# Retention and an exact-GELU MLP on one core: ten warm-up products instead of seven, whole products in the opening's gaps, first loads in another order

## The chip, the core and the metric

The kernel runs on one core of a Trainium2 chip. A core has a matrix engine (TensorE, PE in the profile; its weight loads are listed as PEld), a vector engine (VectorE, DVE), a scalar engine (ScalarE, ACT), a general engine that here mostly issues loads (GpSimd, POOL), and a queue engine for stores (SyncE, SP). They run side by side and wait for each other by semaphores. Sixteen DMA engines move data between the main memory and the core's own memory. The metric is the device time of one execution in microseconds (us), the median of several runs.

## The reference

For 8 batches and 8 heads, 576 positions of 64 numbers, the reference takes retention scores with a decay for each head, multiplies them with the values, lays the heads beside each other, and puts the 4608 rows of 512 through an MLP with an inner width of 2048 and the exact GELU:

```
scores = (1 / sqrt(64)) * q @ k.T                   # per batch and head
gamma  = 1 - 2 ** (-5 - head)
Dmat   = where(i >= j, gamma ** (i - j), 0)
x      = (scores * Dmat) @ v                        # heads side by side: [4608, 512]
h      = x @ w_in                                   # [4608, 2048]
out    = (0.5 * h * (1 + erf(h / sqrt(2)))) @ w_out # [4608, 512]
```

All inputs and the output are float32 in main memory.

## The kernel before

**Tiles.** Positions are cut into pieces of 128 (the fifth has 64), and a unit is one such piece of one batch with all heads. There are 4608 / 128 = 36 units; four make a block of 512 tokens for the MLP, nine blocks in all. The units of the first block, called tiles 0 to 3 here, are the first pieces of batches 0 to 3. A later piece of the same batch needs a state carried over from the pieces before it; the first pieces need none.

**Steps of a unit.** The queries and keys of one unit are transposed on TensorE (`turn`, line 456 for its products) into PSUM and copied out as `qkT` (line 487 on VectorE, 489 on ScalarE). `scores` multiplies them; `masked` (line 623) multiplies the scores in PSUM with the decay (`near`) into `ret`. `inner` multiplies `ret` with the values; `evacuate` converts its result to `x`. `scaled_v` (line 649) weights the values for the carried state, and `state` multiplies them with the keys. `mlp1` multiplies `x` with `w_in` two blocks of 128 inner columns at a time, ScalarE applies the GELU (line 802) into `g_all`, `mlp2` multiplies with `w_out`. Later blocks use a form of both with fewer products. All products go through `mm` (line 452), transposes through `mm_turn` (line 456).

**Opening.** q and k of tile 0 and its values are loaded as float32 by SyncE and ScalarE (line 149) and converted on VectorE (`early<-q`, `early<-k`, `early<-first_v`). All other loads are issued by POOL in the order of the list `ORDER`: in `q1`, `k2` or `v3` the number is the tile, `wi` and `wo` are eighths of `w_in` and `w_out`, `io` builds constants. They land in the tile `early` (line 368), `w_in` (line 311) and `w_out` (line 326). Eight loads are in flight at most; a further one waits until the load eight places ahead of it has landed. The list, as far as it concerns the opening:

```
"wi0 io q1 k2 k1 wi7 v1 q2 k3 v0 wi1 wi6 q3 wo2 v2 wi5 v3 wi3 wi4 wo1 wi2 ..."
```

(`v0` does nothing here, since it came as float32.)

**Warm-up products.** TensorE begins with `N_WARM` products of 128 x 512 on a tile of zeros whose result nobody reads. `warm(n)` puts n more of them where the plan sees a gap. They do no work that the output needs.

**The plan.** The whole program is written out by one loop in Python before it is launched. It keeps a planned time for each engine (`T["pe"]` and so on), planned landing times (`land`) and planned durations, and at each step picks the next piece of work for TensorE that is ready by these times. Nothing of it runs on the chip: only the order it gives does. Four constants that the change touches: `HOT` is the planned time up to which a product counts twice its duration, `WARM_TO` the time up to which gaps are filled, `RATE` says how far scores may run ahead of the MLP, `JOIN` allows scores a little more lead directly after an `inner`. The fill at the loop's end reads:

```
gap = min(waits) - now
if now < WARM_TO and gap > (0.6 if now < HOT else 0.2 if now < 16 else 0.5):
    warm(int(gap / 0.6) + WPLUS if now < HOT else max(1, round(gap / 0.23)) + WPLUS)
```

Of the kernel before, what the change touches and what calls it, by code (L numbers as in the profile page):

```python
# [17 lines left out]
def kernel(  # L18
# [64 lines left out]
    VH_ACT = [4, 22, 1]  # L83
    N_XB = 4
    AHEAD = 13
    RATE = 4.6
    STORE_AT = 62.0
    CROWD = 66.0
    STATE10 = 32.0
    HOT = 7.5  # L90
    FETCH = 5.0
    ARRIVE = 5.6
    WPLUS = 0
    WARM_TO = 24.0
    JOIN = 0
    JOIN_SB = 0.0
    VISIT = 4
    LEAD = 5.0
# [4 lines left out]
    N_V = 6  # L103
    MASK_ACT = 99.0
    V0_HW = 1
    N_WARM = 7
    MSK_AT = 24.0
    HK = N_DF // 2

# [11 lines left out]
    T = dict.fromkeys(("pe", "act", "dve", "pool", "sp"), 0.0)  # L121
# [115 lines left out]
    land = {}  # L237
# [22 lines left out]
    def ring_free(tag):  # L260
        n = RINGS[tag][1]
        return len(taken[tag]) < n or taken[tag][-n]()

    def all_loaded():
        return not ORDER and next_load[0] >= N_G

# [102 lines left out]
            land[what, i] = sw_dma(0.88, 0.9) if j is not None else sw_dma(0.68, 0.5)  # L369

    tiles_of(0)
    land["q", 0], land["k", 0] = 4.65, 5.2
    if V0_HW:
        land["v", 0] = 7.45
    cast_due = {("q", 0): (loaded[0][0][0], first["q32"]), ("k", 0): (loaded[0][0][1], first["k32"])}
    if V0_HW:
        cast_due["v", 0] = (loaded[0][1], first["first_v"])
    ORDER = ("wi0 io q1 k2 k1 wi7 v1 q2 k3 v0 wi1 wi6 q3 wo2 v2 wi5 v3 wi3 wi4 wo1 wi2 wo3 wo0 wo4 wo5 k4 q4 wo7 "
             "q5 wo6 v4 dq2 k5 q6 k7 k6 q7 q8 q9 n4 v6 k8 k9 v8 q10 k11 n8 n6 k10 dq3 q11 q12 v10 dq0 q13 dq4 k12 "
             "k13 n10 n12 v12").split()  # L380

    def next_order():
        item = ORDER.pop(0)
        what = item.rstrip("0123456789")
        load(what, int(item[len(what):] or 0))
# [5 lines left out]
    def reload():  # L391
        if next_load[0] < N_G:
            g = groups[next_load[0]]
            ORDER.extend([f"{what}{i}" for what in "qk" for i in g] + [f"{what}{g[0]}" for what in ("vn" if len(g) > 1 else "v")])
            next_load[0] += 1
# [18 lines left out]
    def bank(shape, dtype, name):  # L414

        now = T["pe"]
        def rank(x):
            y = banks[banks.index(x) ^ 1]
            return free_at[x] > now, y not in held and free_at[y] <= now, free_at[x]
        b = min((x for x in banks if x not in held), key=rank)  # L420
        held.add(b)
        return b, view(b, shape[1:], dtype)
# [19 lines left out]
    def release(b, when):  # L442
        held.remove(b)
        free_at[b] = when
# [5 lines left out]
    def mm(*a, **k):  # L450
        count[0] += 2.004
        nc.tensor.matmul(*a, **k)  # L452
# [5 lines left out]
    def place(n):  # L458
        return (n - 194.0) // 256, (n - 194.0) % 256

    def fetch_at(n):

        at = place(count[0])[1]
        wait = piece[0] + FETCH - (256 - at) * 0.0075 if at + n >= 256 else 0.0
        return 0.0 if T["pe"] < 20.0 else wait
# [4 lines left out]
    def pe(dur, to="full"):  # L470
        if mode[0] != to:
            T["pe"] += 0.05 if mode[0][:4] == to[:4] == "row4" else 0.11
            mode[0] = to
        dur *= 2.0 if T["pe"] < HOT else 1.0
        new, old = place(count[0])[0], place(count[1])[0]
        if new > old:
            turn_at = T["pe"] + dur * (1 - place(count[0])[1] / max(1.0, count[0] - count[1]))
            wait = max(0.0, piece[0] + FETCH - turn_at) if T["pe"] > 20.0 else 0.0
            piece[0] = turn_at + wait
            T["pe"] += wait  # L480
        count[1] = count[0]
        T["pe"] += dur
        return T["pe"] + DRAIN
# [709 lines left out]
    def fire():  # L1193
        now = T["pe"]
        while ORDER and T["pool"] <= now + 1.5:
            next_order()
# [33 lines left out]
    def warm(n):  # L1230
        b, t = bank([128, 512], FP32, "warm")
        for _ in range(n):
            mm(t, lhsT=zeros[:, :128], rhs=zeros, start=True, stop=True)
        pe((0.32 if T["pe"] < HOT else 0.2158) * n)
        release(b, T["pe"])

    def attend(*ns):
# [17 lines left out]
    def s_ready(early=0):  # L1255
        n = group_of[nA]
        g = groups[n]
        if n < nT and n not in [x[0] for x in apart_due] and g[-1] // 4 <= tM1 + N_XB - 1 and nA + len(g) <= AHEAD + early + RATE * b1:
            return sg[n]["T"]
        return 1e9  # L1260
# [7 lines left out]
    T["pe"] = 1.3  # L1268
    for _ in range(N_WARM):
        b, t = bank([128, 512], FP32, "warm")  # L1270
        mm(t, lhsT=zeros[:, :128], rhs=zeros, start=True, stop=True)
        release(b, 0.0)
    T["pe"] = 1.3 + 0.62 * N_WARM
    while True:
        fire()
        now = T["pe"]
# [16 lines left out]
        if nB < nA:  # L1293

            n = group_of[nB]
# [15 lines left out]
        if nA < N_U:  # L1311
            n = group_of[nA]
            g = groups[n]
            if T["dve"] <= now + (SB + JOIN_SB if after_a else SB) and nA - nB <= 2:
                acts.append((max(s_ready(JOIN if after_a else 0), fetch_at(64 if n >= 4 else 0), free_time(0, len(g))), "S"))
        if nT < 4 + NPE and nT <= group_of[min(nA, N_U - 1)] + 3 and (nT < 4 or not half or ring_free("tk")):
# [13 lines left out]
        if due:  # L1330
# [8 lines left out]
            elif kind == "S":  # L1339
                n = group_of[nA]  # L1340
# [40 lines left out]
        if not waits:  # L1381
            break
        gap = min(waits) - now
        if now < WARM_TO and gap > (0.6 if now < HOT else 0.2 if now < 16 else 0.5):
            warm(int(gap / 0.6) + WPLUS if now < HOT else max(1, round(gap / 0.23)) + WPLUS)
        T["pe"] = max(T["pe"], min(waits))
    while stores:
        put()
# [31 lines left out]
```

## Time and profile before

| What | Value |
|---|---|
| median of three runs | 292.75 us |
| the three runs | 293.8, 292.75, 291.52 us |
| profiled execution, first to last instruction (its span) | 288.7 us |
| TensorE busy in the span | 279.1 us (97%) |
| VectorE, ScalarE, POOL busy | 229.5, 178.8, 136.2 us |
| granted TensorE clock, mean of the span | 1.000 |

The profile is of one execution. Its page gives the span from the first to the last instruction and not the whole time of that execution; the runs lie 2.8 to 5.1 us above the span. The rows of a timeline are merged: neighbours of one engine with the same line and tiles stand in one row with their count. In brackets stands how long the engine was idle before the row's first instruction, and what ended that wait. A product's length reaches to its modelled end, so that the lengths of neighbours overlap; the distance of their starts is what they cost in a stream.

### The profile page before, as it was taken

The numbers are of one execution on the slowest core, as the hardware profiler recorded it, in microseconds if no ns is written. First come the engines' busy times: TensorE is split into PE (matmuls) and PEld (weight loads), VectorE is DVE, ScalarE is ACT, GpSimd is POOL, SyncE is SP. The second block draws the span as 40 slices with busy tenths as digits, with TensorE's granted clock in tenths as the row PEclk, the third lists the DMA queues.
The fourth block names the chain that finished last, engine by engine and source line by source line (L and its number), as shares of the span: only waits on it lengthen the run. The fifth ranks groups of instructions, "written<-read, shape, count | busy, mean of one in ns | idle before, by whom it ended". The sixth has DMA issues, their size and how long they took to land.

```text
span 288.7 us, 9727 instructions
## 1 busy us (share of the span) xinstructions
PE 279.1 (97%) x4138; PEld 212.5 (74%) x4162; DVE 229.5 (80%) x384; ACT 178.8 (62%) x400; POOL 136.2 (47%) x205
## 2 busy tenths in 40 slices
PE   6899999999999999999999999999999999999994
PEld 2478767888667766666766766777888888888883
DVE  5564289897964799968996799897996998899861
ACT  7355537998378767778578866655645455555421
POOL 8956868996899777678688820000000000000000
PEclk9999999999999999999999999999999999999999
DMA  9999999999989999999999960302020202101114
GB/s 155 170 183 202 185 163 203 201 124 150 116 98 135 140 169 116 184 133 190 163 122 185 82 104 3 77 2 75 0 75 0 76 3 73 73 2 73 39 55 128
DMA packets 109131, 31.96 MB, mean 111 GB/s; under 512 B 85792, under 2 KB 104736, under 8 KB 109088
## 3 DMA queue, kind: packets, MB, share of 16 engines
q0 software_dynamic: 100400, 21.12, 83.2%
q1 hardware_dynamic: 7264, 9.51, 9.9%
q10 hardware_dynamic: 1424, 0.72, 0.9%
q8 instruction: 32, 0.52, 0.7%
q14 instruction: 11, 0.09, 0.1%
HBM read 42.99 MB, written 9.44 MB: 182 GB/s over the span
## 4 chain that ended last, share of the span: by engine, by line
PE 95%; DMA 2%; issue 1%; DVE 0%; POOL 0%; ACT 0%; POOLq 0%; DVEq 0%
PE psum L452 93%; DMA early<-in_q_dram 2%; PE psum L456 1%; POOL w_in L311 0%; DVE qkT L487 0%; DVE o_sb L884 0%; ACT t L489 0%; POOL val L188 0%; POOLq L188 0%; DVEq L487 0%; POOLq L1404 0%; POOL pos L190 0%
## 5 line engine op out<-in xcount | busy, mean ns | idle before, releaser
L452 PE MATMUL psum<-x,w_in 128*128 128x256 bf16 (+2 forms) x716 | 116.8, 303 | 1.6 <-issue 0.8
L452 PEld LDWEIGHTS <-w_in 128*128 128x128 bf16 x736 | 68.1, 98 | 26.1 <-issue 0.3
L452 PEld LDWEIGHTS <-g_all 128*128 128x128 bf16 x576 | 55.6, 98 | 15.1 <-issue 0.6
L452 PE MATMUL psum<-w_out,g_all 128*128 128x256 bf16 (+1 forms) x438 | 58.6, 280 | 0.0
L799 ACT ACTIVATE g_all<-psum 128x512 bf16<-128x512 f32 x64 | 37.7, 594 | 22.8 <-PE psum L452 22.5
L452 PEld LDWEIGHTS <-s 128*128 128x128 bf16 x408 | 39.3, 98 | 8.5
L346 POOL DMA_DIRECT2D k_ld<-in_k_dram x64 | 35.1, 566 | 18.1 <-DMA q_ld<-in_q_dram 10.3
L645 ACT ACTIVATE vh<-v_ld,dv 128x128 bf16<-128x128 bf16 (+1 forms) x144 | 42.2, 379 | 0.0
L628 DVE TENSOR_TENSOR ret<-psum,msk 128x1024 bf16<-128x1024 f32 (+1 forms) x32 | 35.6, 1150 | 7.3 <-PE psum L452 7.2
L1013 ACT ACTIVATE g_all<-t 128x512 bf16<-128x512 f32 x36 | 22.6, 630 | 29.0 <-DVE t L1021 28.9
L346 POOL DMA_DIRECT2D q_ld<-in_q_dram x64 | 35.3, 570 | 2.0 <-DMA v_ld<-in_v_dram 0.9
L452 PE MATMUL psum<-wt,s 128*128 128x256 bf16 x272 | 34.3, 273 | 0.0
L489 ACT COPY t<-psum 128x256 f32<-128x256 f32 (+1 forms) x46 | 20.0, 436 | 21.8 <-PE psum L452 21.5
L884 DVE TENSOR_TENSOR o_sb<-psum,t 128x256 f32<-128x256 f32 x51 | 21.4, 420 | 12.0 <-ACT t L489 6.3
L1021 DVE TENSOR_TENSOR t<-psum,t 128x512 f32<-128x512 f32 x36 | 24.7, 689 | 6.1 <-ACT t L489 4.2
L487 DVE COPY t<-psum 128x512 f32<-128x512 f32 (+1 forms) x41 | 22.6, 558 | 2.9 <-PE psum L452 2.9
L802 ACT ACTIVATE g_all<-psum 128x512 bf16<-128x512 f32 (+1 forms) x36 | 19.3, 549 | 8.0 <-PE psum L452 7.7
L771 DVE TENSOR_TENSOR x<-psum,dqT 128x1024 bf16<-128x1024 f32 (+1 forms) x18 | 19.4, 1095 | 1.1 <-PE psum L452 1.1
L452 PE MATMUL psum<-x,ws 128*128 128x256 bf16 x144 | 19.5, 273 | 0.0
L357 POOL DMA_DIRECT2D v_ld<-in_v_dram x14 | 16.3, 1167 | 4.0 <-ACT g_all L799 2.0
L452 PE MATMUL psum<-wt,g_all 128*128 128x256 bf16 x136 | 17.5, 273 | 0.5 <-ACT t L489 0.5
L452 PE MATMUL psum<-w_out,s 128*128 128x256 bf16 x136 | 17.5, 273 | 0.0
(100 smaller groups left out, 325.9 us busy)
## 6 DMA issues: line engine op xcount, KB each, us to landing
out_dram<-o_sb SPq DMA_DIRECT2D x31, 256.0 KB, 2.4
v_ld<-in_v_dram POOLq DMA_DIRECT2D x14, 256.0 KB, 5.5
q_ld<-in_q_dram POOLq DMA_DIRECT2D x48, 64.0 KB, 5.1
k_ld<-in_k_dram POOLq DMA_DIRECT2D x48, 64.0 KB, 4.5
kn_ld<-in_k_dram POOLq DMA_DIRECT2D x12, 256.0 KB, 6.1
w_in<-in_moe_w_in_dram POOLq DMA_DIRECT2D x8, 256.0 KB, 8.1
w_out<-in_moe_w_out_dram POOLq DMA_DIRECT2D x8, 256.0 KB, 9.5
k_ld<-in_k_dram POOLq DMA_DIRECT2D x4, 128.0 KB, 7.8
```

Of the source, the lines that this page charges most:

```text
L346: nc.gpsimd.dma_start(qk["qk".index(what)][p0:p0 + 32, 0:HP * per].rearrange("p (h x) -> p h x", h=HP), {"q": q, "k": k}[what][2 * bp + jj ...
L452: nc.tensor.matmul(*a, **k)
L487: nc.vector.tensor_copy(dst, src)
L489: nc.scalar.copy(dst, src)
L628: nc.vector.tensor_tensor(both.rearrange("p (e h) s -> p e h s", e=2), t, by, op=ALU.mult)
L645: nc.scalar.activation(vh[:, 0:m, h], src[:, :, h], AF.Copy, scale=dv[:, h, ci:ci + 1])
L771: nc.vector.tensor_tensor(x.rearrange("p m (j s) -> p j m s", j=2), o, by, op=ALU.mult)
L799: nc.scalar.activation(g_all[:, t % 2, :, m0, :], hT.rearrange("p n (a c) -> p (n a) c", a=2), AF.Gelu)
L802: nc.scalar.activation(g_of(t, 2 * lo // TOK)[:, m0:m0 + n, lo_:lo_ + hi - lo], hT, AF.Gelu)
L884: nc.vector.tensor_tensor(dst, src, f[key], op=ALU.add)
L1013: nc.scalar.activation(g_of(t, part)[:, m0:m0 + 2], src, AF.Gelu)
L1021: nc.vector.tensor_tensor(f[key], f["b"][1], f[key], op=ALU.add)
```

## The change

`N_WARM` goes from 7 to 10, and the plan's time behind these products from 1.3 + 0.62 each to 1.2 + 0.427 each. The planned landings of tile 0's queries and keys move from 4.65 and 5.2 to 5.05 and 5.3. In `warm` the plan counts 0.2158 for a product (twice that before `HOT`, by the factor in `pe`). A gap is filled when it is longer than 0.45 (before `HOT`), 0.25 (up to 16) or 0.5, with as many products as go into it whole, and `WPLUS` and the least of one product are dropped. `HOT` becomes 8.0, `RATE` 4.8, `JOIN` 2. In `ORDER`, `v1` goes behind `q2` and `k3`.

```diff
-    RATE = 4.6
+    RATE = 4.8
...
-    HOT = 7.5
+    HOT = 8.0
...
-    WPLUS = 0
     WARM_TO = 24.0
-    JOIN = 0
+    JOIN = 2
...
-    N_WARM = 7
+    N_WARM = 10
...
-    land["q", 0], land["k", 0] = 4.65, 5.2
+    land["q", 0], land["k", 0] = 5.05, 5.3
...
-    ORDER = ("wi0 io q1 k2 k1 wi7 v1 q2 k3 v0 wi1 wi6 q3 wo2 v2 wi5 v3 wi3 wi4 wo1 wi2 wo3 wo0 wo4 wo5 k4 q4 wo7 "
+    ORDER = ("wi0 io q1 k2 k1 wi7 q2 k3 v1 v0 wi1 wi6 q3 wo2 v2 wi5 v3 wi3 wi4 wo1 wi2 wo3 wo0 wo4 wo5 k4 q4 wo7 "
...
-        pe((0.32 if T["pe"] < HOT else 0.2158) * n)
+        pe(0.2158 * n)
...
-    T["pe"] = 1.3 + 0.62 * N_WARM
+    T["pe"] = 1.2 + 0.427 * N_WARM
...
-        if now < WARM_TO and gap > (0.6 if now < HOT else 0.2 if now < 16 else 0.5):
-            warm(int(gap / 0.6) + WPLUS if now < HOT else max(1, round(gap / 0.23)) + WPLUS)
+        if now < WARM_TO and gap > (0.45 if now < HOT else 0.25 if now < 16 else 0.5):
+            warm(int(gap / (0.45 if now < HOT else 0.23)))
```

In the program that comes out, TensorE's order in the opening is, before (warm-up products as W with their count): 7 W, transposes of tile 0, W, scores 0, transposes of q1, 6 W, `inner` 0, transposes of k1, 3 W, scores 1, MLP, 4 W, transposes of q2, `inner` 1, transposes of k2, `state`, W, MLP, scores 2, MLP, MLP, transposes of tile 3, MLP, scores 3, `inner` 2, 4 W, and so on. After: 10 W, transposes of tile 0, W, scores 0, transposes of q1, 5 W, `inner` 0, transposes of k1, 2 W, MLP, scores 1, transposes of tile 2, 4 W, `inner` 1, scores 2, `state`, MLP, MLP, MLP, transposes of tile 3, MLP, scores 3, `inner` 2, 4 W, and from there on as before.

## Prediction

> **What bounds the kernel now.** I read the page's busy times and chain first, then the chain in order of time, then the timeline of the first 24 us engine by engine, and last the DMA issues in narrow windows.
>
> ```profile
> PE 279.1 (97%) x4138; PEld 212.5 (74%) x4162; DVE 229.5 (80%) x384; ACT 178.8 (62%) x400; POOL 136.2 (47%) x205
> ```
>
> ```profile
> PE 95%; DMA 2%; issue 1%; DVE 0%; POOL 0%; ACT 0%; POOLq 0%; DVEq 0%
> ```
>
> TensorE is busy for 279.1 us, and the chain that ends last is 95% TensorE. So a change in the opening can save no more than the time by which it lets TensorE's unbroken stretch begin sooner. Where does that stretch begin? In the chain in order of time (start, length, what) one piece of 12 us stands at 21.59, the longest so far:
>
> ```profile
> 21.59 12.01 PE psum L452 x140
> ```
>
> From there TensorE hardly waits. Ahead of it the timeline shows TensorE's products (start, length, engine, line, tiles, count, in brackets the idle time before and its releaser):
>
> ```profile
> 1.19 3.17 PE L452 MATMUL psum<-zeros 128*128 128x512 bf16 x7 [1.19 <-DVE zeros L151]
> 5.52 1.04 PE L456 MATMUL psum<-ident,early 128*128 128x128 bf16 x8 [1.16 <-DVE early L487]
> 6.35 0.63 PE L452 MATMUL psum<-zeros 128*128 128x512 bf16 x1
> 7.08 0.61 PE L452 MATMUL psum<-qkT 64*128 64x128 bf16 x8
> 8.37 0.61 PE L456 MATMUL psum<-ident,early 128*128 128x128 bf16 x4 [0.69 <-DMA early<-in_q_dram]
> 8.77 2.77 PE L452 MATMUL psum<-zeros 128*128 128x512 bf16 x6
> 11.47 0.62 PE L452 MATMUL psum<-ret,early 128*32 128x128 bf16 x16
> ...
> 13.83 1.03 PE L452 MATMUL psum<-zeros 128*128 128x512 bf16 x4
> ...
> 15.01 0.41 PE L452 MATMUL psum<-ret,early 128*32 128x128 bf16 x16
> ...
> 17.55 1.92 PE L452 MATMUL psum<-x,w_in 128*128 128x256 bf16 x16
> 19.31 0.61 PE L456 MATMUL psum<-ident,early 128*128 128x128 bf16 x8
> ```
>
> The row of its weight loads at 21.02, and a stage with its granted clock third from the end:
>
> ```profile
> 21.02 0.23 PEld L452 LDWEIGHTS <-early 128*32 128x32 bf16 x16 [0.18 <-DMA early<-in_v_dram]
> ```
>
> ```profile
> 8.40:12.00 3.60, 3.60 (x26) 1.48 (x26) 1.83 (x4) 0.43 (x2) 3.60 (x6) 1.00 2.06 170
> ```
>
> Two things stand here. First, the pace. A warm-up product costs (2.77 - 0.63) / 5 = 0.43 us at 8.77, where 0.63 is the length of a single one (the row at 6.35). At 13.83 it costs about 0.22: one of these, when nothing is slow, takes 0.38 to its end, so (1.03 - 0.38) / 3. I call these the slow and the fast pace; somewhere near 12 us TensorE changed over. The granted clock says 1.00 in a stretch where products ran at the slow pace, so the pace has to be read from durations.
>
> Second, the last wait. The product of tile 2's masked scores with its values (`inner`, at 21.02) was held 0.18 us by the landing of v2, the values loaded for that tile. Two paths meet at 21.0 almost level: TensorE's own work, and v2's landing. The change shortens the first; what it gains is decided by the second.
>
> **The change part by part.** The two programs' instruction orders say what moves. TensorE's order differs only ahead of tile 3's transposes (19.31 above); from there to the end it is the same, instruction for instruction. So RATE 4.8 and JOIN 2 cost and bring nothing outside the opening. On the other engines one conversion (x of tile 1) goes from VectorE to ScalarE, and VectorE's copy of the state moves behind tile 2's two masked products. The warm-up products are 7+1+6+3+4+1+4 before and 10+1+5+2+4+0+4 after: 26 both times, three moved to the front.
>
> *Three more at the front.* 3 x 0.43 = 1.28 us in an idle stretch of 1.16 us (the row at 5.52) that begins when the seventh ends. Counted by starts, ten are issued by 1.19 + 10 x 0.427 = 5.46, and the transposes go at 5.52, released by VectorE's cast. Cost nothing, with 0.06 to spare; without that cover at most 0.1 us, of work that is not on the path at 21.0.
>
> *What they do to the pace.* Before, 3.2 us of products and then an idle stretch did not bring the fast pace; the nearly unbroken work from 8.37 on did, after about 3.7 us. After, work is nearly unbroken from 1.19 to 7.5 (products, transposes, one product, scores). With the same 3.7 us the fast pace comes between 4.9 and about 8, taken here as present from 8.4 on.
>
> *The opening at the fast pace.* Durations are those of the rows above and these (the loads: start of issue, then the time to landing of the one issued at that time):
>
> ```profile
> 7.49 0.63 DVE L487 CAST early<-first_v 128x512 bf16<-128x512 f32 x1 [0.47 <-DMA first_v<-in_v_dram]
> 8.04 1.27 DVE L623 TENSOR_TENSOR ret<-psum,near 128x512 bf16<-128x512 f32 x2
> ...
> 19.80 0.76 DVE L487 COPY qkT<-psum 128x512 bf16<-128x512 bf16 x2 [0.86 <-PE psum L456]
> ```
>
> ```profile
> 6.09 0.90 POOL L368 DMA_DIRECT2D early<-in_v_dram  x1
> 6.96 0.90 POOL L368 DMA_DIRECT2D early<-in_q_dram  x1
> 7.83 0.91 POOL L368 DMA_DIRECT2D early<-in_k_dram  x1
> ...
> 10.18 0.94 POOL L368 DMA_DIRECT2D early<-in_q_dram  x1
> 11.05 0.76 POOL L326 DMA_DIRECT2D w_out<-in_moe_w_out_dram  x1
> 11.74 0.97 POOL L368 DMA_DIRECT2D early<-in_v_dram  x1
> 12.64 0.83 POOL L311 DMA_DIRECT2D w_in<-in_moe_w_in_dram  x1
> ```
>
> ```profile
> early<-in_v_dram POOLq DMA_DIRECT2D x1, 128.0 KB, 6.1
> early<-in_k_dram POOLq DMA_DIRECT2D x1, 128.0 KB, 6.1
> early<-in_q_dram POOLq DMA_DIRECT2D x1, 128.0 KB, 7.2
> w_out<-in_moe_w_out_dram POOLq DMA_DIRECT2D x1, 256.0 KB, 7.6
> early<-in_v_dram POOLq DMA_DIRECT2D x1, 128.0 KB, 9.2
> w_in<-in_moe_w_in_dram POOLq DMA_DIRECT2D x1, 256.0 KB, 9.0
> q8 instruction: 1, 0.02, 5.1%
> q8 instruction: 1, 0.02, 0.2%
> ```
>
> (The six loads are those issued at 6.09, 7.83, 10.18, 11.05, 11.74 and 12.64, in that order. The last two rows count the instruction queue's packets, between 18.9 and 20.1 us, and between 0 and 25.)
>
> The transposes of q1 start at 8.37 as before. Five products at 0.22 end at 9.7; the masked scores are ready at 8.04 + 1.27 = 9.31, which waits for first_v's cast and is not moved. So `inner` of tile 0 runs at 9.7 instead of 11.47: 1.8 us earlier. ScalarE then converts x, and what stands next in TensorE's order (k1's transposes, two products, the first eight of the MLP, the scores of tile 1) is done by about 11.5.
>
> *q2 and k3 ahead of v1.* Three loads of one size (0.90 or 0.91 us of POOL each) change places in POOL's queue; nothing else is passed. v1 now takes k3's place and lands at 7.83 + 6.1 = 13.9 instead of 6.09 + 6.1 = 12.2. Therefore `inner` of tile 1 cannot run before 13.9; before, it ran at 15.01. It is 1.1 us earlier, and v1 has become what it waits for. That is the reordering's whole price, and it is hidden: TensorE has q2's and k2's transposes from 12.2 on (q2 now lands in v1's old place) and four products up to 13.6 in front of it, and the path that decides, v2's, is untouched.
>
> From 13.95: `inner` 0.25, scores of tile 2 0.25, then the state's 32 products once VectorE has scaled v1 (about 0.7 us after v1), ending near 15.05. Sixteen products of 256 columns took 19.31 - 17.55 = 1.76, eight 0.88; three such eights end at 17.7. q3 lands at 10.18 + 7.2 = 17.4, so tile 3's transposes start at 17.7 instead of 19.31: **1.6 us earlier**. Eight products (0.45) and VectorE's two copies (0.76) later, the scores of tile 3 end near 19.25. There TensorE waits for v2. If ScalarE is late (its gelus now stand behind x of tile 1 and behind a copy of the state that waits for VectorE), up to 1.1 us of it vanishes in that wait, more shows.
>
> *v2.* Its place in POOL's queue is the same. w_out lands at 11.05 + 7.6 = 18.6, v2 at 11.74 + 9.2 = 21.0, the next w_in at 12.64 + 9.0 = 21.7. So v2 came 2.3 us after its predecessor and w_in only 0.7 after v2. How long would they take alone? From v1 to k3, two loads of v2's size went by in 13.9 - 12.2, 0.87 each; from q3 to w_out, one of w_in's size in 18.6 - 17.4 = 1.2. By this v2 was due at 19.5 and w_in at 20.7: v2 came 1.5 late, w_in 0.9. In exactly this stretch a packet of the instruction queue was moved, the only one of the first 25 us. I take it that this fetch sat in front of v2's last part on one of the sixteen DMA engines; it is an inference from the coincidence. TensorE's position in its program draws the fetch, so after the change it should come some 1.6 us sooner, hit an earlier load, and leave v2 the smaller delay: 19.5 + 0.9 = 20.4 instead of 21.0. The bounds: v2 as late as before (gain 0), or v2 unhindered (gain min(1.5, 21.02 - 19.25) = 1.5). I take **0.6**, between the ends, because the load behind v2 shows the 0.9.
>
> After 21.0 all is the same work in the same order. The sum against the profiled execution: 288.7 - 0.6 = 288.1. What lies around the span isn't on the page; the runs lie 2.8 to 5.1 above it, the median 292.75 by 4.05. With the same surround: 292.15, rounded 292.2.
>
> **The rivals.**
>
> *A. v2 lands as before.* TensorE arrives 1.8 us early and waits it out. For it: v2's place and bytes are the same. Span 288.7, time 292.8.
>
> *B. v2 lands unhindered*, because the fetch comes early enough for its engine to catch up: span 287.2, time 291.25.
>
> *C. The ten products don't bring the fast pace.* What counts as work is not shown: 3.2 us and a gap did not do. If the transposes and small scores between 5.5 and 7.5 don't count, only 4.3 us of products are left against 3.7, and a late turn of up to 12 us is possible again. The five products would cost 2.15 instead of 1.08, `inner` of tile 0 would run at 11.0, tile 3's transposes near 18.7 and the scores by 20.3, still before 21.0. Price: between nothing and A's wait; time 292.2 to 292.8. The Trainium skill, "TensorE: Matmul & The Clock Gate", "Part 4: PE-mode transpose", says that transposes don't count as busy work for the clock in the usual way. That speaks for C; without that rule the forecast stands, and no row here separates the two.
>
> *D. The slower one: the pace falls back.* Case A or the forecast leave TensorE idle from 19.25 to 20.4 or 21.0, with little work in the 3.4 us around. If a stretch that is mostly idle takes the fast pace away, the next 3.7 us run at half speed: 3.7 / 2 = 1.85 us lost, span 288.1 + 1.85 = 290.0, time 294.0. It decides from how long the wait for v2 is; against it, the wait is 1.8 us at most. The same page of the Trainium skill, in "Why this matters for your kernels", gives gaps beyond about 3 us between bursts as what brings the slow clock back; by it D would not happen. In the profile TensorE has no such stretch between the opening and its end, so nothing here shows it.
>
> **How the numbers follow.** Forecast, with C's share that ends alike (292.2): 0.50. A: 0.23. B: 0.11. D: 0.13. The rest, 0.03, is what I haven't seen. The three runs of before spread by 2.3 us, so a median of such runs moves by about 1 to either side; The range reaches from a little under B to D: 290.6 to 294.0, which leaves out about 2 in 10. One per cent (2.9 us) is about what a measurement of this kernel can tell from no change. No case reaches it alone; B with a lucky median gives 0.05 faster, D with an unlucky one 0.06 slower, 0.89 lie within.
>
> **What would show it.** In the profile after: warm-up products near 0.22 at 8.6 instead of 0.43; `inner` of tile 0 near 9.7; `inner` of tile 1 at 13.9 with v1 as its releaser; tile 3's transposes near 17.7; a wait of 1 to 1.8 us on v2 ahead of tile 2's `inner`, which itself is between 20.3 and 21.0; the instruction packet near 17 us. I am wrong if tile 2's `inner` runs before 19.8 or after 21.4, if products after it take twice their time, or if a wait appears after 25 us that the present chain lacks.

## The result, and the profile after

The changed kernel takes 290.09 us, the median of 15 executions (289.63 to 290.94); the kernel before, measured beside it, 291.39 (15 executions, 290.0 to 293.8). The ratio is **0.9959, with a 95% interval from 0.9941 to 0.9977**: a small gain, 1.3 us in this comparison. In all executions that were made for this study the changed kernel has a median of 290.39 (37 executions) and the one before 291.37 (158 executions), 1.0 us apart.

| | before | after |
|---|---|---|
| median beside each other, us | 291.39 | 290.09 |
| span of the profiled execution, us | 288.7 | 288.7 |
| span, median of all executions, us | 289.6 (288.2 to 293.5) | 288.6 (287.9 to 289.9) |
| time less span, us | 1.73 to 1.87 | 1.73 to 1.84 |

The spans of before are of 143 executions, those of the changed kernel of 37. Over all kernels of this study the time less the span is 1.73 to 1.89 in 311 of 314 executions; the other three, at 2.05 to 3.04, are of the two kernels with split products below. The second row shows a trap: the two profiled executions have the same span, and yet the kernels differ. The profile of before came from one of its quicker executions: 21 of 143 have a span of 288.7 or less.

The page of the changed kernel, busy times and the shares of the chain that ended last:

```profile
PE 279.6 (97%) x4162; PEld 211.7 (73%) x4162; DVE 229.5 (80%) x383; ACT 179.1 (62%) x401; POOL 135.9 (47%) x205
...
PE 91%; POOL 4%; DMA 3%; issue 0%; DVE 0%; ACT 0%; POOLq 0%
```

TensorE's share of the chain fell from 95 to 91%, because the chain now begins with POOL's loads and a DMA. The same chain in order of time (start, length, what) shows where it passes to TensorE:

```profile
11.73 8.62 DMA early<-in_v_dram
20.34 0.04 issue
20.39 17.13 PE psum L451 x208
...
47.39 89.65 PE psum L451 x1740
137.04 0.53 issue
137.56 147.36 PE psum L451 x1895
```

v2's landing is on the path, and TensorE's long stretch begins at 20.39 instead of 21.02 (21.59 in the chain of before is the start of a piece of the same stretch). One more thing stands here that the chain of before did not have: 0.53 us at 137 us in which TensorE waited for nothing that the profile shows. Instruction for instruction, the profiled execution is 0.63 us ahead of before's from 21 to 136 us and level with it from there on, so this one wait cost it the whole gain of the opening.

The opening on TensorE, in the columns of the prediction (lines are one lower than before: L451 is `mm`, L455 `mm_turn`):

```profile
1.19 4.45 PE L451 MATMUL psum<-zeros 128*128 128x512 bf16 x10 [1.19 <-DVE zeros L150]
...
8.51 0.40 PE L455 MATMUL psum<-ident,early 128*128 128x128 bf16 x4 [0.92 <-DMA early<-in_q_dram]
8.74 1.24 PE L451 MATMUL psum<-zeros 128*128 128x512 bf16 x5
9.91 0.41 PE L451 MATMUL psum<-ret,early 128*32 128x128 bf16 x16
...
11.49 0.62 PE L451 MATMUL psum<-x,w_in 128*128 128x128 bf16 x8 [0.41 <-DMA w_in<-in_moe_w_in_dram]
...
13.99 0.41 PE L451 MATMUL psum<-ret,early 128*32 128x128 bf16 x16
...
18.38 0.61 PE L455 MATMUL psum<-ident,early 128*128 128x128 bf16 x8 [0.51 <-ACT g_all L801]
18.82 0.61 PE L451 MATMUL psum<-x,w_in 128*128 128x128 bf16 x8
19.68 0.40 PE L451 MATMUL psum<-qkT 64*128 64x128 bf16 x8 [0.25 <-DVE qkT L486]
20.39 0.41 PE L451 MATMUL psum<-ret,early 128*32 128x128 bf16 x16 [0.31 <-DMA early<-in_v_dram]
```

The fast pace is there at 8.51: four transposes end after 0.40 instead of 0.61, and five products take 1.24 where six took 2.77. `inner` of tile 0 runs at 9.91 (before 11.47), of tile 1 at 13.99 (15.01), of tile 2 at 20.39 (21.02), where it waits for v2.

### The profile page after: what moved, and what is told of

It reads as the page before. It is cut to its first block, busy times and chain, and to the rows that moved or that the text cites. A ratio compares the mean times of both kernels' runs of the same rounds, so it can differ in the third digit from the quotient of the medians.

```text
span 288.7 us, 9750 instructions
## 1 busy us (share of the span) xinstructions
PE 279.6 (97%) x4162; PEld 211.7 (73%) x4162; DVE 229.5 (80%) x383; ACT 179.1 (62%) x401; POOL 135.9 (47%) x205
## 4 chain that ended last, share of the span: by engine, by line
PE 91%; POOL 4%; DMA 3%; issue 0%; DVE 0%; ACT 0%; POOLq 0%
PE psum L451 91%; DMA early<-in_v_dram 3%; POOL early L367 2%; POOL w_in L310 1%; PE psum L455 1%; POOL w_out L325 0%; DVE o_sb L883 0%; ACT t L488 0%; POOL val L187 0%; POOL pos L189 0%; POOLq L187 0%; POOLq L1403 0%
## 5 line engine op out<-in xcount | busy, mean ns | idle before, releaser
L451 PE MATMUL psum<-x,w_in 128*128 128x256 bf16 (+2 forms) x736 | 118.9, 305 | 0.4 <-DMA w_in<-in_moe_w_in_dram 0.4
L451 PEld LDWEIGHTS <-w_in 128*128 128x128 bf16 x736 | 68.1, 98 | 26.7 <-DMA w_in<-in_moe_w_in_dram 0.9
L451 PEld LDWEIGHTS <-g_all 128*128 128x128 bf16 x576 | 55.6, 98 | 15.1 <-issue 0.6
L451 PE MATMUL psum<-w_out,g_all 128*128 128x256 bf16 (+1 forms) x440 | 59.0, 280 | 0.0
L451 PEld LDWEIGHTS <-s 128*128 128x128 bf16 x408 | 39.3, 98 | 8.6
L451 PE MATMUL psum<-wt,s 128*128 128x256 bf16 x272 | 34.3, 273 | 0.0
L801 ACT ACTIVATE g_all<-psum 128x512 bf16<-128x512 f32 (+1 forms) x36 | 19.1, 550 | 7.3 <-PE psum L451 7.0
L451 PE MATMUL psum<-x,ws 128*128 128x256 bf16 x144 | 19.5, 273 | 0.0
L451 PE MATMUL psum<-wt,g_all 128*128 128x256 bf16 x136 | 17.5, 273 | 0.5 <-ACT t L488 0.5
L451 PE MATMUL psum<-w_out,s 128*128 128x256 bf16 x136 | 17.5, 273 | 0.0
```

The lines of the kernel that those rows point to most:

```text
L801: nc.scalar.activation(g_of(t, 2 * lo // TOK)[:, m0:m0 + n, lo_:lo_ + hi - lo], hT, AF.Gelu)
```

## The experiments

Each kernel ran beside the kernel before, whose medians in these comparisons were 290.94 to 291.46. "`inner` 2" is the start of tile 2's `inner` in the profile of one execution. A "fallen" execution is one whose mean clock is 0.9955 or less: one stretch of 3.41 us at half clock takes 3.41 / 2 / 289 = 0.6% off the mean, and the end of the kernel takes at most another 0.3%. A fall says that the fast pace had been there and was lost for a piece: the time before it first comes isn't in the clock's records and doesn't count.

| kernel | median us (executions) | ratio to before, 95% | `inner` 2 | fallen |
|---|---|---|---|---|
| after | 290.09 (15) | 0.9941 to 0.9977 | 20.39 | 2 of 15 |
| ten_moved | 290.2 (12) | 0.9953 to 0.9995 | 20.29 | 2 of 12 |
| after_seven | 291.86 (12) | 1.0007 to 1.0057 | 21.79 | 6 of 12 |
| before_again | 291.35 (12) | 0.9973 to 1.0024 | 21.44 | 3 of 12 |
| after_v2swap | 290.31 (12) | 0.9951 to 0.9986 | 20.70 | 5 of 12 |
| six_to_three | 291.46 (12) | 0.9975 to 1.0018 | 20.32 | 3 of 12 |
| ten_six | 290.53 (12) | 0.9954 to 0.9991 | 20.42 | 4 of 12 |
| after_fill | 290.6 (12) | 0.9951 to 0.9988 | 20.43 | 0 of 12 |
| fill_v2swap | 290.2 (12) | 0.9943 to 0.9988 | 19.99 | 0 of 12 |
| after_again | 290.43 (10) | 0.9940 to 0.9987 | 20.41 | 0 of 10 |
| after_old_loads | 290.46 (10) | 0.9949 to 0.9994 | 20.65 | 1 of 10 |
| after_split | 294.17 (4) | 1.0066 to 1.0154 | 20.24 | 1 of 4 |
| split_same_plan | 297.92 (4) | 1.0161 to 1.0267 | 20.67 | 3 of 4 |
| fetch53 | 290.9 (10) | 0.9985 to 1.0032 | 20.76 | 4 of 10 |
| fetch56 | 291.27 (10) | 0.9988 to 1.0029 | 20.76 | 5 of 10 |
| after_b | 290.77 (12) | 0.9951 to 0.9994 | 20.45 | 1 of 12 |
| fill_v2swap_b | 290.5 (12) | 0.9951 to 0.9999 | 20.40 | 0 of 12 |

### Which part of the change earns the time

**ten_moved**: the kernel before with nothing but three products moved to the front.

```diff
-        for _ in range(n):
+        for _ in range(3 if n == 6 else n):
...
-    for _ in range(N_WARM):
+    for _ in range(10):
```

> The kernel before, with one edit: ten warm-up products in front, and three instead of six behind q1's transposes; the plan and every other instruction stay. Theory 1 (the pace): the ten products alone bring the fast pace by 8 us, tile 0's inner moves from 11.5 to about 9.5, tile 2's inner waits for v2 and runs near 20.4, and the whole gain is there: ratio to before 0.994 to 0.998, runs within 1.5 us of each other. Rival 2 (the plan): the gain needs the new fills and the reordered loads; then the ratio is 0.998 to 1.0 and the runs spread as those of before (3.8 us).

290.2, nearly the whole gain; `inner` 2 at 20.29. The runs spread by 2.0 us, more than the 1.5 that I had expected.

**after_seven**: the changed kernel with seven products in front.

```diff
-    for _ in range(N_WARM):
+    for _ in range(7):
...
+    count[0] += 3 * 2.004
```

> The changed kernel with seven products in front again, all else as changed. Theory 1: the slow pace lasts to about 12 us as before, tile 0's inner runs near 11, tile 2's inner between 20.4 and 21.5, and the executions spread again by over 2 us; ratio to before 0.998 to 1.002. Rival 2: without the three products the changed plan keeps most of the gain: ratio 0.995 to 0.997 and a spread under 1.5 us.

The gain is gone and a little more: 291.86, slower than before by 0.07 to 0.57%. The fast pace came at 13.69 us, and `inner` 2 ran at 21.79, later than I had expected.

**ten_six** and **six_to_three** take the two halves of ten_moved apart: ten in front with the six kept, and seven in front with three in place of the six.

```diff
-    for _ in range(N_WARM):
+    for _ in range(10):
...
+    count[0] -= 3 * 2.004
```

> The kernel before with ten products in front and all six kept behind q1's transposes; nothing else. Theory 1: at the fast pace the six cost 1.3 us and end near 9.9, tile 0's inner is about 1.5 us earlier than before, tile 2's inner near 20.4, ratio 0.995 to 0.998. Rival 3: no gain without the three fewer, ratio 0.999 to 1.001.

```diff
-        for _ in range(n):
+        for _ in range(3 if n == 6 else n):
...
+        count[0] += 3 * 2.004 * (n == 6)
```

> The kernel before with three instead of six warm-up products behind q1's transposes and seven in front as before; every other instruction in its place. It splits the two halves of ten_moved. Theory 1 (the pace): without the three in front the slow pace still lasts to 12 us or beyond; the path is three slow products shorter (1.28 us), but the later change of pace gives part of it back: ratio 0.997 to 1.0, a spread of the runs over 2 us as before, tile 2's inner between 20.4 and 21.5. Rival 3 (a shorter path): ten_moved gained only because three slow products left the path; then the ratio is 0.995 to 0.9975 and the spread under 2 us.

Ten in front alone give 290.53; the shorter path alone gives 291.46, no gain. So the gain belongs to the ten products. `inner` 2 in six_to_three's profile is as early as after's, for two reasons: the path is shorter, and in this execution seven products did bring the fast pace, at 4.80. It was lost for a piece at 8.21, as the rows show:

```profile
7.18 0.40 PE L452 MATMUL psum<-qkT 64*128 64x128 bf16 x8 [0.30 <-DVE qkT L487]
8.58 0.61 PE L456 MATMUL psum<-ident,early 128*128 128x128 bf16 x4 [1.00 <-DMA early<-in_q_dram]
8.99 1.49 PE L452 MATMUL psum<-zeros 128*128 128x512 bf16 x3
```

Then two losses follow: this execution waited 0.51 us at 50 and 1.32 us at 139 us for nothing shown, and its span is 290.2. So with seven products the early pace is there in some executions and not in others. Of the 143 executions of before, 51 have fallen, and for a fall the fast pace must have been there; their spans have a median of 289.1, those of the other 92 one of 289.7. In after_seven it is 289.5 for the six fallen and 290.5 for the other six. The program is the same on both sides of these two comparisons, so they speak for the pace as what the ten products earn the time by. Where in those executions the fall came isn't on record.

**after_old_loads**: the changed kernel with v1, q2 and k3 loaded in the places they had before, TensorE's order unchanged.

```diff
+        first_places = {("q", 2): ("v", 1), ("k", 3): ("q", 2), ("v", 1): ("k", 3)}
+        if (what, i) in first_places:
+            w2, i2 = first_places[what, i]
...
```

> The changed kernel with q2, k3 and v1 loaded in the places they had before (v1 first), TensorE's order unchanged. My theory, that v2's landing alone decides: v1 lands near 12.2 instead of 13.9, q2 near 13.1; TensorE now waits for q2 ahead of tile 2's transposes, and `inner` of tile 1 runs at 13.9 to 14.4, tile 3's transposes at 18.3 to 18.8, and `inner` of tile 2 at 20.3 to 20.6, since v2's place is the same. Time within 0.4 of the changed kernel in this call. Rival: moving v1 back is part of what the change earns; then `inner` of tile 2 is later than 20.8 and the time 290.6 or more.

The median, 290.46, is that of the changed kernel beside it (after_again, 290.43). TensorE waited 0.92 us for q2, `inner` of tile 1 ran at 14.64 and tile 3's transposes at 19.02, each 0.2 later than the latest I had expected, and `inner` 2 at 20.65, which waited for no load. The order of the loads is worth 0.26 us in the opening of this profile and nothing that the time shows.

### What v2's landing decides

**after_v2swap**: the changed kernel with v2 loaded ahead of the second eighth of w_out.

```diff
+        if (what, i) == ("wo", 2):
+            nc.gpsimd.dma_start(v0_, v[2 * units[2][0] + units[2][2], :, 0:C, :].rearrange("h s d -> s h d"))
...
+        if (what, i) == ("v", 2):
+            nc.gpsimd.dma_start(w_out[:, 4:6, :], moe_w_out[512:768, :].rearrange("(c p) f -> p c f", p=128))
...
```

> The changed kernel with the loads of v2 and of the second eighth of w_out in each other's place in POOL's queue; every other engine's order is the same. If v2's landing is what sets the start of the unbroken stretch, v2 lands near 19.3 (the instruction packet's delay included), tile 2's inner runs right behind tile 3's scores near 19.95 instead of 20.4, and spans and median fall by about 0.4 us against the changed kernel (ratio to before 0.993 to 0.996). If a later wait takes such a gain back, as near 137 us in the changed kernel's profile, inner runs near 19.95 and the median stays at the changed kernel's (ratio 0.9955 to 0.997).

v2 landed at 18.22 and nothing waited for it, but the profiled execution lost the pace in the opening, its `inner` 2 ran at 20.70 where I had expected 19.95, and the median, 290.31, is not below after's. Its TensorE rows, and the windows (length, busy times of PE, PEld, DVE, ACT and POOL with counts, granted clock, DMA share, GB/s):

```profile
8.40 0.60 PE L464 MATMUL psum<-ident,early 128*128 128x128 bf16 x4 [1.24 <-DMA early<-in_q_dram]
8.79 2.34 PE L460 MATMUL psum<-zeros 128*128 128x512 bf16 x5
```

```profile
5.03:8.44 3.41, 1.75 (x20) 0.78 (x19) 2.68 (x6) 3.39 (x8) 3.41 (x5) 1.00 1.91 178
8.44:11.86 3.42, 3.42 (x28) 1.55 (x29) 1.79 (x4) 0.52 (x3) 3.42 (x5) 0.50 2.04 171
11.86:15.27 3.41, 3.36 (x57) 2.18 (x55) 2.31 (x4) 2.05 (x5) 3.24 (x5) 1.00 1.85 181
```

The clock is granted in pieces of 3.41 us. After one in which TensorE was busy for 1.75 us, with 1.24 us of idle time in one stretch ahead of q1, the next was granted at half: the five products cost 2.34 again. In the profile of after, the piece at the same place held:

```profile
5.65:9.06 3.41, 1.87 (x23) 1.08 (x22) 3.25 (x6) 3.16 (x7) 3.41 (x5) 1.00 2.11 168
9.06:12.48 3.42, 3.01 (x45) 1.54 (x43) 1.46 (x5) 0.92 (x2) 3.36 (x5) 1.00 2.05 170
```

**before_again**, the kernel before once more.

> The kernel before once more, for the spans of its executions. If the profiled execution of before (288.7) was one of its fast ones, most spans here are over 289.2 with a median near 289.6, and a profile of a longer one shows the slow pace lasting beyond 12.2 us and tile 2's inner after 21.1. If instead the time around the span varies, the spans stay near 288.7 and the times spread by more than they do.

Here the instruction packet came at 19.32, behind v2, which landed at 19.68 and held nobody up; the next w_in landed late, at 21.80. Over the profiles a packet that starts at 16.15 to 16.61 delays q3, at 17.28 to 18.24 w_out (in after, at 17.73: w_out landed at 19.80, of which 15 of 16 parts were there at 18.74), at 18.93 v2 (before), and at 19.32 or 19.62 the w_in behind it; the one in fetch53 at 18.25 delays v2. TensorE's place in its program draws the packet, and what it delays is the load that is landing then. TensorE's rows of this execution:

```profile
8.98 2.77 PE L452 MATMUL psum<-zeros 128*128 128x512 bf16 x6
...
13.01 0.59 PE L452 MATMUL psum<-zeros 128*128 128x512 bf16 x2 [0.18 <-issue]
...
21.44 0.41 PE L452 MATMUL psum<-ret,early 128*32 128x128 bf16 x16
```

`inner` 2 came 0.42 us later than in before's first profile though v2 was early: its pace had changed at 12.95 instead of 12.15, and TensorE's own work was the bound. The span was 289.7, like the median of all executions of before (289.6), and of the 1.0 us between this execution and the first, the opening is 0.3 to 0.4; 0.46 were lost in one step at 99.5 us and 0.25 in another at 160.

### Keeping the pace while TensorE waits for q1

**after_fill**: three products more between the scores of tile 0 and q1's transposes. **fill_v2swap**: the same, with v2 ahead of w_out.

```diff
+        if nT == 1 and half == 0:
+            b, t = bank([128, 512], FP32, "warm")
+            for _ in range(3):
+                nc.tensor.matmul(t, lhsT=zeros[:, :128], rhs=zeros, start=True, stop=True)
+            held.remove(b)
         turn(nT, half)
```

> The changed kernel with three more products between tile 0's scores and q1's transposes, where TensorE waits for q1 for about 1.2 us; nothing else. If that idle stretch is what made the granted clock fall back for one window in 9 of 39 executions with ten in front (mean clock 0.991 to 0.995, at span medians 0.4 to 0.8 us longer), no execution here has a mean clock under 0.996, and the median is 0 to 0.2 us under the changed kernel's (ratio to before 0.9945 to 0.9965). If the fall has another cause, the same share of executions shows it.

> The same three products in after_v2swap, where v2 is loaded ahead of w_out. There no load covers TensorE's own work any more, so a fall of the clock costs all it takes: with the fill tile 2's inner runs near 19.95 in every execution, the median is 0.2 to 0.5 us under after_v2swap's 290.31, and this is the quickest version (ratio 0.993 to 0.996). If the wait at the instruction packet near 137 us sets a floor, inner runs near 19.95 and the median stays at 290.0 to 290.3.

No execution fell, 0 of 36 with after's opening, the three products and either order of v2 (with fill_v2swap_b below); of the kernels with ten in front and nothing in this gap 24 of 103 did. That share differs much from one comparison to the next, 0 of 10 for after_again and 9 of 20 for fetch53 and fetch56, whose openings are the same. Beside each other ran ten_six with 4 of 12 and the two with three more products with 0 of 24. But the median didn't follow: 290.6 and 290.2. after_fill lost 0.57 us at 50 us, again without a releaser. fill_v2swap's profile has the earliest `inner` 2 of all, 19.99, but by 49 us all but 0.02 of its 0.39 us of lead over after's was lost. It passed 137 us without after's wait and was then 0.8 ahead; at 142 it lost 0.6 of that at one instruction, and its span is 288.5. Beside the changed kernel:

> The changed kernel unchanged, as the measure for the run beside it. 289.9 to 290.5; some executions in ten have a lower mean clock (up to four), since the wait for q1 can still cost the fast pace; these are 0.5 to 1.5 us longer.

> The changed kernel with three more products in the wait for q1 and v2 loaded ahead of wo2 (as in the earlier run of it), now beside the changed kernel in one call. If the three products keep the pace, no execution has a mean clock of 0.9955 or less, and the median lies 0.1 to 0.5 below the changed kernel's, more the more of that kernel's executions fell. Rival: the gain at 21 us is taken back at the pieces' turns, whose places moved by 6; then the medians are level within 0.15 or this is slower.

290.77 and 290.5. after_b is above the 290.5 that I had expected at most. In fill_v2swap_b the packet came at 16.61 and q3 landed at 18.71, so that `inner` 2 ran at 20.40 although v2 was there at 19.20. The difference has the sign and size that I expected, but one execution in 12 of the changed kernel fell here, too few to explain it, and the two ranges (289.92 to 291.69, 289.59 to 291.7) lie over each other: it is not shown that this version beats the changed kernel.

### The waits without a releaser behind 25 us

**after_again**, the changed kernel once more.

> The changed kernel once more, unchanged: what differs from its first profile is not the change. If the 0.53 us that TensorE lost at 137 us belongs to the program, it stands there again. If it hangs on when a packet of the instruction queue happens to come, as I hold, the profile has a stall of 0.2 to 0.6 us at none, one or two of the places where a piece of 256 instructions ends (50, 99, 137 us), not always the same. Opening: `inner` of tile 2 at 20.3 to 20.5. Time 289.9 to 290.4; two executions in fifteen or so with a lower mean clock.

```profile
50.04 0.36 PE L451 MATMUL psum<-q_ld,u_sb 32*64 32x128 bf16 x12 [0.40 <-issue]
...
137.79 0.43 PE L451 MATMUL psum<-vh,kn_ld 128*32 128x64 bf16 x33 [0.23 <-issue]
```

The wait at 137 is there again, at the same instruction and half as long; one at 50 and one at 160 (0.20) have joined it. The plan in the kernel counts pieces of 256 instructions (`place`), so I counted too. In after, the wait at 137 stands at instruction 4531 = 17 x 256 + 179; in after_again that at 50 stands at 1211 = 4 x 256 + 187.

**after_split** was to move these places: each of the ten products cut into four of 128 columns, 60 instructions more.

```diff
-        mm(t, lhsT=zeros[:, :128], rhs=zeros, start=True, stop=True)
+        for c4 in range(0, 512, 128):
+            mm(t[:, c4:c4 + 128], lhsT=zeros[:, :128], rhs=zeros[:, c4:c4 + 128], start=True, stop=True)
```

> The changed kernel with each of the ten products in front cut into four of 128 columns: the same columns, 60 instructions more, so every later instruction stands 60 places further in TensorE's program. If the stalls behind 25 us stand where a piece of 256 instructions ends, those of this profile (none to two, 0.2 to 0.6 us each) stand again at instruction 208 + k x 256 of its own program, which is 60 places earlier in the work than before, and not between the 31st and 32nd product of the `state` at 137 us. Rival: the stall belongs to that `state` (a tile it waits for); then it stands in the same group as in the changed kernel. Opening: fast pace at 5.0 to 6.5, the first instruction packet sooner than 17.7, `inner` of tile 2 at 20.2 to 20.6. Time 289.8 to 290.6.

294.17, far outside. But the run doesn't answer cleanly: the plan counts TensorE's instructions, and with 60 more it wrote another order. **split_same_plan** keeps the plan's count and so the order:

```diff
+        count[0] += 2.004
         for c4 in range(0, 512, 128):
-            mm(t[:, c4:c4 + 128], lhsT=zeros[:, :128], rhs=zeros[:, c4:c4 + 128], start=True, stop=True)
+            nc.tensor.matmul(t[:, c4:c4 + 128], lhsT=zeros[:, :128], rhs=zeros[:, c4:c4 + 128], start=True, stop=True)
```

> The changed kernel with each of the ten products in front cut into four of 128 columns, not counted by the plan: TensorE's order after them is that of the changed kernel, instruction for instruction, but each stands 60 places further in the program. (In the run before this, the plan counted them and wrote another order.) If TensorE's stalls behind 25 us come where a piece of 256 instructions ends, at 208 + k x 256, those of this profile stand 60 places earlier in the work than in the changed kernel, none in the middle of the `state` at 137 us, and since the plan places its work for the old ends, there are more of them: 0.5 to 2 us in all, time 290.5 to 292. Rival: the stall at 137 us belongs to that `state` and its tiles; then it stands there again, and the time is 289.8 to 290.6. Opening as in the changed kernel: `inner` of tile 2 at 20.2 to 20.6.

297.92 (295.57 to 300.84): the same work in the same order, 60 places further in the program, costs 5 to 10 us against the changed kernel's 290.39. The direction was as I expected, the size some four times the most that I had expected. The profiled execution is the longest of the four, so its waits show where the time goes and not how much of it is usual. TensorE's rows around 140 us in this kernel, and its windows there:

```profile
138.97 0.70 PE L451 MATMUL psum<-vh,kn_ld 128*32 128x64 bf16 x64
139.60 1.08 PE L451 MATMUL psum<-q_ld,u_sb 32*64 32x128 bf16 x64
140.62 0.28 PE L451 MATMUL psum<-w_out,g_all 128*128 128x256 bf16 x1
144.26 2.08 PE L451 MATMUL psum<-w_out,g_all 128*128 128x256 bf16 x9 [3.36 <-issue]
```

```profile
140.50:143.91 3.41, 0.40 (x17) 0.14 (x6) 2.54 (x3) 1.27 (x2) 1.80 (x4) 1.00 2.20 160
143.91:147.32 3.41, 3.06 (x15) 2.20 (x15) 0.00 (x0) 0.89 (x2) 2.51 (x4) 0.50 1.02 125
```

The `state` with `kn_ld`, in which after waits, runs through its 64 products; the wait has gone to the next `mlp2`, 3.36 us long, and took the pace with it for the piece behind. The chain of this kernel names the others, behind 25 us:

```profile
58.67 1.14 issue
...
112.58 0.57 issue
...
140.90 3.36 issue
...
168.23 1.50 issue
...
193.00 0.62 issue
```

These are 7.19 us together. In the 18 profiles of this study there are 26 waits of at least 0.2 us behind 25 us that nothing shown ended; **all 26 stand 179 to 187 instructions into a piece of 256**, whatever work is there, and in all 26 TensorE goes on 1.24 to 1.59 us after a packet of the instruction queue has ended. So they belong to the packets and not to the work. If the profile's few semaphore instructions on TensorE are counted too, all 26 stand at 193 or 194, and 194 is where the plan's `place` begins its pieces. The first profile of before has none of them. The second, before_again, has none that is listed so, but its two steps at 99.5 and 160 us stand 187 and 179 instructions into their pieces, 1.33 and 1.49 us behind a packet, and fill_v2swap's loss at 142 stands at 181, 1.48 behind one. So the kernel before pays for these turns too.

**fetch53** and **fetch56**: the plan allows for these turns (`FETCH` = 5.0 is its least time between two of them); here with 5.3 and with 5.6.

```diff
-    FETCH = 5.0
+    FETCH = 5.3
```

> The changed kernel with the plan told that two pieces of 256 instructions can't follow each other in less than 5.3 us, instead of 5.0; its order differs from about instruction 2850 on, in some 400 places. If the turns of the pieces take back part of the opening's gain, this has fewer or shorter stalls behind 60 us, and the time is 289.6 to 290.2, spans mostly 287.9 to 288.4. Rival: the stalls hang on when packets happen to come and not on the plan's distance, or the new order costs as much as it saves; then 290.1 to 290.8 with stalls as before.

> As the run before, with 5.6 us; the order differs from about instruction 2100 on, in some 700 places. If 5.0 is too short because packets come up to 3 us after the turn and TensorE goes on 1.5 us after them, this has no stall at a piece's end behind 45 us and 289.5 to 290.2. Rival: the plan now puts waits of its own, or an order that costs VectorE or ScalarE more, in the place of the stalls: 290.3 to 291.5.

290.9 and 291.27: no gain, and both at or a little above what the rivals gave. fetch53's profile has none of these waits and still a span of 289.1, since this execution fell in the opening (products 2.12 instead of 1.24 at 8.68). Its new order made its lag behind after's profile grow from 0.4 to up to 1.7 us between 94 and 140 us, and from 153 on it is 0.4 again. fetch56 still has two waits, 0.42 and 0.49. Many executions of both fell, but those that didn't have median spans of 289.1 and 289.5, above after's 288.6 as well.

## Why the prediction was wrong, point by point

The forecast was 292.2 with a range down to 290.6; measured is 290.09, below the range.

**The step that failed is the last of the sum, "What lies around the span".** I took the distance between three executions and the span of a fourth, 4.05 us, for something that surrounds every execution. Measured with the span of the same execution it is 1.73 to 1.89. The rest of the 4.05 was spread: before's executions have spans of 288.2 to 293.5 with a median of 289.6, the profile showed a quick one, and the three runs were slower ones than the 15 measured beside the changed kernel (292.75; the 15, which include the three, have 291.39). With 1.8 in its place the forecast's own span of 288.1 gives 289.9, beside 290.09 measured; the changed kernel's spans have a median of 288.3 in these 15 executions and 288.6 in all 37. That 288.1 is so near them is in part luck: it starts from a span 0.9 below the median of before and takes off too little.

**So the gain was mis-sized too: 0.6 forecast, 1.0 to 1.3 measured.** 0.63 is right between the two profiles (21.02 and 20.39). Between the second ones (21.44 and 20.41) it is 1.03. That a typical execution of before loses more, since its fast pace comes later than in the one I priced, is read from two profiles of before and three of the changed kernel (20.39, 20.41, 20.45) together with the median spans, 289.6 and 288.6. Of the other executions only the mean clock is known; that the fallen ones of before are 0.6 shorter (under six_to_three, above) fits it.

**Ten products cost nothing in front and bring the fast pace: right.** The transposes still go at 5.51. It is there from 8.4 on, as taken, and ten_six shows that they alone earn the time. C falls: the five products cost 1.17 (from 8.74 to `inner` 0 at 9.91), not 2.15. Only in fallen executions do they cost as much, and these had the fast pace before. Whether transposes count as work for the pace isn't decided: the products alone nearly fill the piece ahead of the fast pace in after's three profiles. Two readings of mine in this part were too simple. In six_to_three's profile seven products did bring the pace. And the 1.00 that I read in the stretch from 8.40 to 12.00 was no record of a clock: the records of that execution begin at 12.15.

**The opening: right up to tile 1, 0.7 late behind it.** `inner` 0 at 9.91 (9.7), `inner` 1 at 13.99 (13.9 to 13.95). Tile 3's transposes ran at 18.38 where 17.7 stood in the sum: this is the wait for ScalarE's gelu at L801, of which 0.51 us show as idle time. ScalarE was held by the copy of the state at 16.75, which waited for VectorE, as I had allowed for with up to 1.1 us. A wait of 0.41 for the eighth of w_in ahead of the MLP at 11.49 I had not seen, because before no product needed it so early; it cost nothing, since `inner` 1 ran 0.04 us behind v1's landing at 13.95. What was late is hidden by the wait for v2, which was 0.31 us long and not 1 to 1.8.

**v2: right, mechanism and size.** The packet came at 17.73 ("near 17"), hit w_out, and v2 landed at 20.34 (forecast 20.4, bounds 19.5 and 21.0). Its parts bear out the reading: 15 of 16 were there at 19.59, and in before's profile, where it landed at 20.98, at 19.45. That was one execution; the packet's place varies, and in before_again it missed v2 altogether.

**A** falls (v2 at 20.34 and not 21.0). **B** falls too: its 291.25 came nearest to the time, but v2 was not unhindered. **D**, the rival on the other side, did not happen where I put it, in the wait for v2, but it does happen: in 24 of 103 executions of the kernels with ten products in front, in the wait for q1 where profiles show it (after_v2swap, fetch53 and fetch56, at 8.44 to 8.89), and in split_same_plan after 3.36 us of idle time. There it cost 1.4 us (TensorE's lag against after's profile grew from 5.19 to 6.61 in that piece), where I had 1.85. In the opening it costs 0.9 (289.2 against 288.3 in the spans of after_v2swap, fallen and not); why less wasn't tried. I had it decided by the length of one wait, and that was the wrong measure: in the opening the falls go with how much of a 3.41 us piece TensorE works (last section). The Trainium skill, "TensorE: Matmul & The Clock Gate", "Why this matters for your kernels", warns of gaps beyond about 3 us; here a piece with one gap of 1.24 us lost the pace (after_v2swap, above), so the measurement decides against that figure as a safe bound.

**"A wait appears after 25 us that the present chain lacks":** it does, 0.53 at 137, and takes the profiled execution's gain back to nothing: 288.7 both times. I had "after 21.0 all is the same work in the same order", which is true and isn't enough: the packets of instructions don't come at the same distance from the work each time.

## What to carry to other kernels

A span and a time belong together only when they are of the same execution: a forecast made against one profile needs to know where that execution lies among the others, and the surround has to be measured, not taken from other runs. Where the pace of TensorE depends on how full a stretch of a few us is, products that nobody reads can keep it over an early wait as well as bring it; that this saved time is not shown here. And the position of an instruction in TensorE's program is a resource like any other: adding instructions early can move every later fetch to a worse place, so a change in their number is to be compared with the number kept, as this change did with 26 and 26.

## What the hardware showed that I had not expected

**The pace and how full a piece is.** By the pieces of 3.41 us in the records, TensorE went over to the fast pace after pieces in which it was busy 81% or more (after 76% and less it did not), and in the opening lost it after pieces with 41, 52, 54 and 54%, but not with 55, 59, 60 and more; the piece with the wait of 3.36 us in split_same_plan had 12%. The busy times contain modelled ends, so an edge near 55% would be good to a few per cent. And the busy share alone doesn't settle it: at the end of two kernels pieces with 45% (fetch56, from 285.03) and 47% (six_to_three, from 284.70) were followed by one at full clock. What sets them apart from the opening's was not tried. The phase of these pieces differs between executions of the same kernel (fast from 4.41, 4.39 and 5.65 in three of the changed kernel), and with it whether the wait for q1 falls into one piece.

**The turn of an instruction piece can cost 0.2 to 3.4 us.** The Trainium skill, "Runtime: NRT & Kernel Launch", "Instruction fetch mechanics", calls the crossing of a block of 256 instructions mostly hidden; in most of the 32 pieces here it is, and the trace agrees so far, but the 26 waits above are not, and 60 places of shift made 7.19 us of waits in one execution of a kernel of 290. What sets how late a packet comes is not settled: in the changed kernel the one for the wait at 137 us came 2.73 us after TensorE had crossed into the piece before, in the profile of before 1.74, with the same loads and stores nearby. That it shares its DMA engines with them was argued and not tried.
